# A planner's durations set anew, and five key chunks moved from VectorE to ScalarE, in a 32-head attention kernel

## The chip, the core and the metric

One core of one Trainium2 chip. The metric is the device time of one execution in microseconds; of several executions, the median. The profiled execution is one more, with a time of its own.

## What is computed

Attention over 32 heads with 2048 queries and 2048 keys of 20 numbers each, where queries and keys are brought to unit length first and each head has its own temperature `t`:

```python
qn = q / (jnp.sqrt((q * q).sum(axis=-1, keepdims=True)) + eps)
kn = k / (jnp.sqrt((k * k).sum(axis=-1, keepdims=True)) + eps)
logits = jnp.einsum('bhqd,bhkd->bhqk', qn, kn) * t[None, :, None, None]
attn = _softmax(logits, axis=-1)
return jnp.einsum('bhqk,bhkd->bhqd', attn, v)      # q, k, v: (1, 32, 2048, 20) bf16
```

Logits are bounded by `t`, about 1, so the exponential needs no maximum taken off first. A column of ones beside V gives the softmax's sum.

## The kernel before

**Tiles.** The 2048 keys of a head are 16 chunks of 128 keys; the 2048 queries are 4 groups of 512. A unit is one chunk by one query group: a logit tile of 128 x 512 in one PSUM bank. The exponential of a unit is made in one of two ways, and `DVE_TILES` says for how many of a head's 16 chunks each is used (3 and 4 by turns, so 3.5 on average go to VectorE).

**ScalarE's way** (`add_wave`, L406 on). Three units make a wave: TensorE computes its three logit tiles into one half of `psA` (task `qkA`), and one ACTIVATE of 128 x 1536 (L429, task `exp`) writes the exponentials to the ring `p_ring`, which holds 36 units. `psA` has two halves, so the logits of a wave may be computed once the ACTIVATE two waves back has ended. Of a wave's three matmuls the first two use 64 rows of the array each and run side by side; the third uses 128 rows.

**VectorE's way** (`add_dtile`, L444 on). One chunk, four query groups. Four times, TensorE computes one logit tile into `psD`, a single bank (task `qkD`), and VectorE turns it into 16-bit integers (task `t1`, L457, tile `xt`); `psD` is free for the next only then. After that VectorE makes from the whole `xt` (128 x 2048) the three parts of an approximate exponential: `ee` (L462), `ss` (L465), and `mm` then `tt` (L467, L470). TensorE multiplies all three by V.

**Output.** For four units (one chunk) TensorE adds V times the exponentials into `psO`: four matmuls of 32 columns side by side (L378; tasks `pvA` from the ring, `pvE`, `pvS`, `pvT` from VectorE's tiles). `psO` is one bank for all heads: when a head's products are all in, VectorE transposes it (`tr`, L387), and only then may the next head's first product be issued. VectorE divides by the sum (L391, L392), SyncE stores.

**Preparation.** For each head VectorE squares, sums, takes a reciprocal root and scales (L286 to L308), SyncE transposes and copies with DMAs.

**What sets the order.** All work is a list of tasks, each with an engine, a duration in us, its predecessors and a priority (lower is sooner). `Program.schedule` plays the list in time: an engine that is free takes the ready task of the lowest priority number, and holds it for its duration; a successor on another engine becomes ready after `SEM_LAT` of the engine it waits for. The order found is then fixed: each engine issues its tasks in it, and waits on semaphores where a task needs another engine. So a duration in that list does no work on the chip; it only decides what stands ahead of what. Waves have the priority `due - 100`, `qkD` `due - 50`, `t1` `due - 5`, V products and the rest about `due`, where due is counted in heads.

Durations before, for the tasks that the change touches: a wave's logits `0.22 * max(1, len(us) - 1)` = 0.44, a `psD` tile 0.22, a V product `PE_GROUP` = 0.27, an ACTIVATE `0.093 + n / 1200` = 1.373, the three large preparation steps 0.75 each.

Of the kernel before, what the change touches and what calls it, by code (L numbers as in the profile page):

```python
# [14 lines left out]
ACT = mybir.ActivationFunctionType  # L15
# [24 lines left out]
class Program:  # L40

    SEM_LAT = {"PE": 0.20, "ACT": 0.15, "DVE": 0.10, "POOL": 0.15, "SP": 0.0}

    def __init__(self):
        self.tasks = []
# [5 lines left out]

    def schedule(self):
        for t in self.tasks:
            t.n, t.users = 0, []
        for i, t in enumerate(self.tasks):
            t.seq = i
            t.deps = list(dict.fromkeys(t.deps))
            t.n = len(t.deps)  # L60
            for d in t.deps:
                d.users.append(t)
        free = {}
        ready = {}
        events = []
        rt = {}

        def arrive(t, when):
            heapq.heappush(events, (when, 0, t.seq, t))

        for t in self.tasks:
            free.setdefault(t.eng, 0.0)
            ready.setdefault(t.eng, [])
            rt[t.seq] = 0.0
            if t.n == 0:
                arrive(t, 0.0)
        order = {e: [] for e in free}
        done = 0
        while events:
            now = events[0][0]  # L80
            touched = set()
            while events and events[0][0] <= now:
                _, kind, _, t = heapq.heappop(events)
                touched.add(t.eng)
                if kind == 0:
                    heapq.heappush(ready[t.eng], (t.pri, t.seq, t))
            for e in touched:
                if free[e] > now + 1e-9 or not ready[e]:
                    continue
                _, _, t = heapq.heappop(ready[e])  # L90
                t.start = now
                t.end = now + t.dur
                free[e] = t.end
                order[e].append(t)
                done += 1
                heapq.heappush(events, (t.end, 1, t.seq, t))
                for u in t.users:
                    lat = t.lat if t.dma else (0.0 if u.eng == e and e != "DVE" else self.SEM_LAT[e])
                    rt[u.seq] = max(rt[u.seq], t.end + lat)
                    u.n -= 1  # L100
                    if u.n == 0:
                        arrive(u, rt[u.seq])
        assert done == len(self.tasks), "dependence cycle"
        self.order = order
        return order
# [57 lines left out]
def bass_standalone__qk_norm__prompt_kernel(  # L163
# [7 lines left out]
    B, H, S, D = q.shape  # L171
    assert B == 1 and D == 20 and S == 2048, (B, H, S, D)
    R = S // 128
# [3 lines left out]
    NB = 4  # L177
    NT = 3
    NX = 3
    DVE_TILES = [4 if h % 2 else 3 for h in range(H)]  # L180
    WPLAIN = 5
    PE_GROUP = 0.27
    SH_ENG, SH_DUR = "DVE", 0.60

    with ExitStack() as es:
# [78 lines left out]
        def add_prep(h):  # L264
            b, b2, bt = h % NB, h % 2, h % NT
            due = h - 2.2
            war = ([norm[h - NB]] if h >= NB else []) + ([trn[h - 2]] if h >= 2 else [])
            lds = []
            for nh in range(4):
                src = bass.AP(q.tensor, q[0, h].offset + nh * D,  # L270
                              [[16 * D, 32], [4 * D, 4], [512 * D, 4], [1, D]])
                dst = qk_sb[b][32 * nh:32 * nh + 32, 0:R, :].rearrange("p (c g) d -> p c g d", g=4)
                lds.append(add("ACT" if h == 0 and nh >= 2 else "SP", f"ldq{h}", lambda eng, tk, dst=dst, src=src: eng.dma_start(dst, src),
                               0.6, war, due - 0.5 + 0.01 * (nh >= 2), lat=2.5, dma=f"q{b}a" if h == 0 and nh >= 2 else f"q{b}"))
            src_k = k[0, h].rearrange("(p r) d -> p r d", p=128)
            lds.append(add("SP", f"ldk{h}", lambda eng, tk: eng.dma_start(qk_sb[b][:, R:2 * R, :], src_k),
                           0.6, war, due - 0.51, lat=2.5, dma=f"k{b}"))
            src_v = v[0, h].rearrange("(p r) d -> p r d", p=128)
            warv = pv_users[h - NB] if h >= NB else z_v[b]
            ld_v[h] = add("SP", f"ldv{h}", lambda eng, tk: eng.dma_start(vaug[b][:, :, 0:D], src_v),  # L280
                          0.6, warv, due - 0.4, lat=3.0, dma=f"v{b}")

            def dv(name, fn, dur, deps):
                return add("DVE", name + str(h), fn, dur, deps, due)
            x = qk_sb[b]
            c = [dv("sq", lambda eng, tk: eng.tensor_tensor(sq[:, :, :], x[:, :, :], x[:, :, :], ALU.mult),  # L286
                    0.75, lds + prep_deps)]
            c.append(dv("sum", lambda eng, tk: eng.tensor_reduce(rs["sum"][:, :], sq[:, :, :], AXIS_X, ALU.add),  # L288
                        0.75, [c[-1]]))
            c.append(dv("rs", lambda eng, tk: eng.tensor_scalar(  # L290
                rs["u"][:, :].bitcast(I32), rs["sum"][:, :].bitcast(I32), -0.5, 1597463007.0, ALU.mult, ALU.add),
                0.12, [c[-1]]))
            cur = rs["u"]
            for tgt in (rs["y"], rs["r"]):
                c.append(dv("rs", lambda eng, tk, cur=cur: eng.tensor_tensor(  # L295
                    rs["a"][:, :], cur[:, :], cur[:, :], ALU.mult), 0.12, [c[-1]]))
                c.append(dv("rs", lambda eng, tk: eng.scalar_tensor_tensor(  # L297
                    rs["b"][:, :], rs["a"][:, :], -0.5, rs["sum"][:, :], ALU.mult, ALU.mult), 0.12, [c[-1]]))
                c.append(dv("rs", lambda eng, tk, cur=cur, tgt=tgt: eng.scalar_tensor_tensor(
                    tgt[:, :], rs["b"][:, :], 1.5, cur[:, :], ALU.add, ALU.mult), 0.12, [c[-1]]))  # L300
                cur = tgt
            c.append(dv("rs", lambda eng, tk: eng.tensor_scalar(
                rs["r"][:, 0:R], rs["r"][:, 0:R], t_f32[:, h:h + 1], None, ALU.mult), 0.12, [c[-1], tcp]))
            if h == 0:
                first_head(x, c[-1])
                return
            war = [trn[h - 2]] if h >= 2 else [z_qkn[b2]]
            norm[h] = dv("norm", lambda eng, tk: eng.tensor_tensor(  # L308
                qkn[b2][:, :, 0:D], x[:, :, :], bc(rs["r"][:, :], 2 * R), ALU.mult), 0.75, [c[-1]] + war)
            prep_deps[:] = [norm[h]]  # L310

            war = (qk_users[h - NT] + [*rot[h - NT]] + (qz0 if h == NT else [])) if h >= NT else []
            trn[h] = add("SP", f"trn{h}", lambda eng, tk: eng.dma_start_transpose(
                qkT[bt][:, :].rearrange("p (c n) -> p c n", n=128),
                qkn[b2][:, :, :].rearrange("p r d -> p (r d)")), 0.1, [norm[h]] + war, due + 0.1,
                lat=3.0, dma=f"T{bt}")
            rot[h] = []
            for g in range(NG):
                rot[h].append(add("SP", f"qz{h}", lambda eng, tk, g=g: eng.dma_start(
                    qz[bt][32 * g:32 * g + 32, g, :], qkT[bt][32 * g:32 * g + 32, 0:512]), 0.6,  # L320
                    [trn[h], z_qz[bt]], due + 0.15, lat=2.0, dma=f"Z{bt}"))
            for dl in range(1, 4):
                n = 128 - 32 * dl
                for (d0, s0, m) in ((0, 32 * dl, n), (n, 0, 32 * dl)):
                    rot[h].append(add("SP", f"rot{h}", lambda eng, tk, d0=d0, s0=s0, m=m, dl=dl: eng.dma_start(
                        kR[bt][d0:d0 + m, dl - 1, :], qkT[bt][s0:s0 + m, 512:1024]), 0.6, [trn[h]], due + 0.2,
                        lat=2.0, dma=f"R{bt}"))
# [78 lines left out]
        def add_wave(w):  # L406
# [13 lines left out]
            deps = [act.get(w - 2)]  # L420
            for h in hs:
                deps += [trn[h]] + (rot[h] if w else rot[h][:1]) + (qz0 if w >= WPLAIN and h == 0 else [])
            qk = add("PE", f"qkA{w}", f_qk, 0.22 * max(1, len(us) - 1), deps, due_a(us[0]) - 100)
            for h in hs:
                qk_users[h].append(qk)
            p0 = us[0] % NP
# [1 line left out]
            war = [pv_of_group[(u - NP) // 4] for u in us if u >= NP]  # L428
            act[w] = add("ACT", f"exp{w}", lambda eng, tk: eng.activation(  # L429
                p_ring[:, p0 * 512:p0 * 512 + n], psA[:, slot * WAVE * 512:slot * WAVE * 512 + n], ACT.Exp),  # L430
                0.093 + n / 1200.0, [qk] + war, 0)

        def add_group(i):
            us = list(range(4 * i, 4 * i + 4))
# [9 lines left out]
        def add_dtile(j):  # L444
# [7 lines left out]
            for ii in range(NG):  # L452
                g = NG - 1 - ii
                dep = [trn[h]] + rot[h] + [t1_prev[0]] + (qz0 if h == 0 and j > 0 else [])
                qk = add("PE", f"qkD{j}.{g}", lambda eng, tk, g=g: qk_mm(eng, h, r, g, psD[:, :], 32 if j == 0 else 128), 0.22, dep, due - 50)
                qk_users[h].append(qk)
                t1 = add("DVE", f"t1.{j}.{g}", lambda eng, tk, g=g: eng.tensor_scalar(  # L457
                    xt[s][:, 512 * g:512 * g + 512], psD[:, :], X_MUL, X_ADD, ALU.mult, ALU.add), 0.60,
# [103 lines left out]
```

## Time and profile before

| | |
|---|---|
| median of 2 runs | 788.19 us (788.02 to 788.36) |
| the profiled execution's own time | 787.52 us |
| its span (first to last instruction) | 785.4 us |
| granted TensorE clock | 0.996 of full |
| PE (TensorE matmul) busy | 718.6 us, 91% |
| DVE (VectorE) busy | 752.7 us, 96% |
| ACT (ScalarE) busy | 736.4 us, 94% |
| DMA engines' mean busy share, 100 to 200 us | 0.30 |

A profile's row names the engine, the line, the operation and the tiles. Two instructions of one engine overlap in it: the next may start before the one before has been acknowledged. So the start-to-start distance of two neighbours (here called the pitch) is shorter than the duration of one, and a busy sum, in which overlaps count once, holds a little waiting that no row calls idle. A matmul's row is its latency; its pitch is less.

### The profile page before, as it was taken

The page shows a single profiled execution, that of the slowest core. Times are in us where ns is not written, and L with a number is a line of the kernel's source. Part 1 is how long each engine was busy: PE and PEld are TensorE (multiplying, and loading weights), DVE is VectorE, ACT ScalarE, POOL GpSimd, SP SyncE. Part 2 cuts the span into 40 slices and gives each one's busy share as a digit, 9 for nine tenths or more (in the row PEclk, how much of TensorE's full clock was granted, in tenths as well). Part 3 has the DMA queues.
Part 4 walks back from the last instruction along what each step waited for, and adds up shares of the span by engine and source line. Part 5 has one row for each costly group of instructions (what it writes and reads, how often), then busy time and mean ns, then how long its engine had stood idle before and what let it go on. Part 6 is the DMA issues. An engine that isn't in the chain of part 4 may idle for free.

```text
span 785.4 us, 12656 instructions
## 1 busy us (share of the span) xinstructions
PE 718.6 (91%) x4992; PEld 201.1 (26%) x4992; DVE 752.7 (96%) x1355; ACT 736.4 (94%) x536; POOL 5.5 (1%) x16
## 2 busy tenths in 40 slices
PE   0999999999999999999999999999999999999996
PEld 0222222222222222222222222222222222222221
DVE  6799999999999999999999999999999999999998
ACT  1899999999999999999999999999999999999994
POOL 2000000000000000000000000000000000000000
PEclk9999999999999999999999999999999999999998
DMA  7324132232323233132332323223232331321100
GB/s 82 50 40 71 42 52 40 46 52 54 55 38 47 43 53 58 40 53 28 57 53 50 54 31 58 41 50 59 30 53 45 54 58 32 46 43 44 42 5 9
DMA packets 199466, 36.49 MB, mean 46 GB/s; under 512 B 175216, under 2 KB 199408, under 8 KB 199408
## 3 DMA queue, kind: packets, MB, share of 16 engines
q1 hardware_dynamic: 198352, 35.66, 28.0%
q8 instruction: 39, 0.64, 0.3%
q10 hardware_dynamic: 1056, 0.04, 0.1%
q14 instruction: 19, 0.16, 0.1%
HBM read 7.87 MB, written 2.62 MB: 13 GB/s over the span
## 4 chain that ended last, share of the span: by engine, by line
DVE 58%; PE 37%; issue 3%; DMA 1%; SPq 0%; DVEq 0%
DVE xt L457 23%; PE psA L369 16%; PE psO L378 14%; DVE tt L470 12%; PE psD L369 8%; DVE mm L467 6%; DVE ss L465 5%; DVE ee L462 4%; DVE sq L286 2%; DVE qkn L308 2%; DVE o_stage L392 1%; DVE oT L387 1%; DVE rs_a L295 1%; DVE rs_sum L288 1%; DVE rs_b L297 1%
## 5 line engine op out<-in xcount | busy, mean ns | idle before, releaser
L429 ACT ACTIVATE p_ring<-psA 128x1536 bf16<-128x1536 f32 x534 | 734.9, 1457 | 37.4 <-PE psA L369 32.5
L457 DVE TENSOR_SCALAR xt<-psD 128x512 int16<-128x512 f32 x448 | 307.7, 687 | 27.3 <-PE psD L369 22.4
L369 PE MATMUL psA<-qz,kR 64*128 64x512 bf16 (+1 forms) x1189 | 314.0, 389 | 1.2 <-ACT p_ring L429 0.2
L378 PE MATMUL psO<-p_ring,vaug 128*32 128x512 bf16 x1600 | 145.4, 387 | 2.5 <-DVE oT L387 2.4
L369 PE MATMUL psD<-qz,kR 128*128 128x512 bf16 x333 | 129.2, 388 | 17.9 <-DVE xt L457 14.1
L470 DVE TENSOR_TENSOR tt<-xt,mm 128x2048 f16<-128x2048 f16 x112 | 136.5, 1219 | 0.1
L369 PEld LDWEIGHTS psA<-qz,kR 64*128 64x128 bf16 (+1 forms) x1189 | 82.1, 94 | 196.3 <-issue 162.1
L369 PE MATMUL psA<-qz,qkT 64*128 64x512 bf16 (+1 forms) x396 | 129.9, 388 | 0.3
L462 DVE TENSOR_SCALAR ee<-xt 128x2048 int16<-128x2048 int16 x112 | 77.0, 687 | 0.2
L465 DVE TENSOR_SCALAR ss<-xt 128x2048 int16<-128x2048 int16 x112 | 77.1, 688 | 0.0
L467 DVE TENSOR_SCALAR mm<-xt 128x2048 int16<-128x2048 int16 x112 | 76.9, 687 | 0.0
L369 PEld LDWEIGHTS psD<-qz,kR 128*128 128x128 bf16 x333 | 32.0, 96 | 98.2 <-DVE xt L457 72.1
L378 PEld LDWEIGHTS psO<-p_ring,vaug 128*32 128x32 bf16 x1600 | 36.6, 94 | 75.3 <-issue 63.2
L378 PE MATMUL psO<-tt,vaug 128*32 128x512 f16 x448 | 44.8, 390 | 8.0 <-DVE tt L470 3.6
L369 PE MATMUL psD<-qz,qkT 128*128 128x512 bf16 x111 | 43.0, 388 | 7.6 <-DVE xt L457 5.2
L378 PE MATMUL psO<-ee,vaug 128*32 128x512 f16 x448 | 44.7, 389 | 3.7 <-DVE ee L462 3.4
L378 PE MATMUL psO<-ss,vaug 128*32 128x512 f16 x448 | 44.8, 390 | 3.4 <-DVE ss L465 2.4
L369 PEld LDWEIGHTS psA<-qz,qkT 64*128 64x128 bf16 (+1 forms) x396 | 31.5, 94 | 63.7 <-issue 52.6
L286 DVE TENSOR_TENSOR sq<-qk_sb 128x640 f32<-128x640 bf16 x32 | 26.0, 813 | 0.1
L288 DVE TENSOR_REDUCE rs_sum<-sq 128x32 f32<-128x640 f32 x32 | 25.7, 804 | 0.1
L308 DVE TENSOR_TENSOR qkn<-qk_sb,rs_r 128x640 bf16<-128x640 bf16 x31 | 25.3, 816 | 0.0
L387 DVE STREAM_TRANSPOSE oT<-psO 128x512 f32<-128x512 f32 x32 | 22.7, 711 | 0.7 <-PE psO L378 0.7
(37 smaller groups left out, 136.6 us busy)
## 6 DMA issues: line engine op xcount, KB each, us to landing
kR<-qkT SPq DMA_DIRECT2D x62, 96.0 KB, 2.1
qz<-qkT SPq DMA_DIRECT2D x128, 32.0 KB, 1.9
kR<-qkT SPq DMA_DIRECT2D x62, 64.0 KB, 2.0
qk_sb<-in_k_dram SPq DMA_DIRECT2D x32, 80.0 KB, 2.1
vaug<-in_v_dram SPq DMA_DIRECT2D x32, 80.0 KB, 3.3
out_dram<-o_stage SPq DMA_DIRECT2D x32, 80.0 KB, 1.6
qk_sb<-in_q_dram SPq DMA_DIRECT2D x126, 20.0 KB, 2.5
kR<-qkT SPq DMA_DIRECT2D x62, 32.0 KB, 1.9
```

The lines of the kernel that those rows point to most:

```text
L286: c = [dv("sq", lambda eng, tk: eng.tensor_tensor(sq[:, :, :], x[:, :, :], x[:, :, :], ALU.mult), 0.75, lds + prep_deps)]
L288: c.append(dv("sum", lambda eng, tk: eng.tensor_reduce(rs["sum"][:, :], sq[:, :, :], AXIS_X, ALU.add), 0.75, [c[-1]]))
L308: norm[h] = dv("norm", lambda eng, tk: eng.tensor_tensor(qkn[b2][:, :, 0:D], x[:, :, :], bc(rs["r"][:, :], 2 * R), ALU.mult), 0.75, [c[-1] ...
L369: return eng.matmul(dst, lhsT, mov, tile_position=(p0, 0))
L378: last = eng.matmul(psO[32 * g:32 * g + 32, :], lhsT(g), rhs_of(g), start=start, stop=False, skip_group_check=True, tile_position=(0, 32 * g))
L387: tr = add("DVE", f"tr{h}", lambda eng, tk: eng.transpose(oT[:, :, :].rearrange("p r d -> p (r d)"), psO[:, :]), 0.62, pv_users[h] + ([fin ...
L429: act[w] = add("ACT", f"exp{w}", lambda eng, tk: eng.activation(p_ring[:, p0 * 512:p0 * 512 + n], psA[:, slot * WAVE * 512:slot * WAVE * 5 ...
L457: t1 = add("DVE", f"t1.{j}.{g}", lambda eng, tk, g=g: eng.tensor_scalar(xt[s][:, 512 * g:512 * g + 512], psD[:, :], X_MUL, X_ADD, ALU.mult ...
L462: te = add("DVE", f"e{j}", lambda eng, tk: eng.tensor_scalar(ee[s][:, :], xt[s][:, :], 0x7C00, KE_BITS, ALU.bitwise_and, ALU.bitwise_or), ...
L465: t5 = add(SH_ENG, f"s{j}", lambda eng, tk: eng.tensor_scalar(ss[s][:, :], xt[s][:, :], float(SHIFT - 4096), None, ALU.add), SH_DUR, t1s + ...
L467: tm = add("DVE", f"m{j}", lambda eng, tk: eng.tensor_scalar(mm[s2][:, :], xt[s][:, :], 0x3FF, 0x3800, ALU.bitwise_and, ALU.bitwise_or), 0.60,
L470: tT = add("DVE", f"T{j}", lambda eng, tk: eng.tensor_tensor(tt[s][:, :], xt[s][:, :].bitcast(FP16), mm[s2][:, :].bitcast(FP16), ALU.mult) ...
```

## The change

Three VectorE chunks in two of three heads and four in the third (heads 1, 4, ... 31) instead of three and four by turns: 107 chunks in place of 112 on VectorE, 405 in place of 400 on ScalarE. All other edits are durations of the planner: a wave's logits 0.55 (0.24 in the first five waves), a `psD` tile 0.24, a V product 0.23, and 0.09 more for a TensorE task that is of another kind than the one before it, where kind is the first two letters of the task's name (`qk` or `pv`); an ACTIVATE `0.065 + n / 1200` = 1.345; the three large preparation steps 0.86; TensorE's latency 0.18. A predecessor may now be a function that gives a list; no task has one.

```diff
-    SEM_LAT = {"PE": 0.20, "ACT": 0.15, "DVE": 0.10, "POOL": 0.15, "SP": 0.0}
+    SEM_LAT = {"PE": 0.18, "ACT": 0.15, "DVE": 0.10, "POOL": 0.15, "SP": 0.0}
...
-            t.deps = list(dict.fromkeys(t.deps))
+            deps = []
+            for d in t.deps:
+                deps += d() if callable(d) else [d]
+            t.deps = list(dict.fromkeys(deps))
...
+        last_pe = [""]
...
                 t.end = now + t.dur
+                if e == "PE":
+                    kind = t.name[:2]
+                    if kind != last_pe[0]:
+                        t.end += 0.09
+                    last_pe[0] = kind
                 free[e] = t.end
...
-    DVE_TILES = [4 if h % 2 else 3 for h in range(H)]
+    DVE_TILES = [4 if h % 3 == 1 else 3 for h in range(H)]
     WPLAIN = 5
-    PE_GROUP = 0.27
+    PE_GROUP = 0.23
...
             c = [dv("sq", lambda eng, tk: eng.tensor_tensor(sq[:, :, :], x[:, :, :], x[:, :, :], ALU.mult),
-                    0.75, lds + prep_deps)]
+                    0.86, lds + prep_deps)]
             c.append(dv("sum", lambda eng, tk: eng.tensor_reduce(rs["sum"][:, :], sq[:, :, :], AXIS_X, ALU.add),
-                        0.75, [c[-1]]))
+                        0.86, [c[-1]]))
...
-                qkn[b2][:, :, 0:D], x[:, :, :], bc(rs["r"][:, :], 2 * R), ALU.mult), 0.75, [c[-1]] + war)
+                qkn[b2][:, :, 0:D], x[:, :, :], bc(rs["r"][:, :], 2 * R), ALU.mult), 0.86, [c[-1]] + war)
...
-            qk = add("PE", f"qkA{w}", f_qk, 0.22 * max(1, len(us) - 1), deps, due_a(us[0]) - 100)
+            qk = add("PE", f"qkA{w}", f_qk, 0.24 if w < WPLAIN else 0.55 if len(us) > 1 else 0.24, deps, due_a(us[0]) - 100)
...
-                0.093 + n / 1200.0, [qk] + war, 0)
+                0.065 + n / 1200.0, [qk] + war, 0)
...
-                qk = add("PE", f"qkD{j}.{g}", lambda eng, tk, g=g: qk_mm(eng, h, r, g, psD[:, :], 32 if j == 0 else 128), 0.22, dep, due - 50)
+                qk = add("PE", f"qkD{j}.{g}", lambda eng, tk, g=g: qk_mm(eng, h, r, g, psD[:, :], 32 if j == 0 else 128), 0.24, dep, due - 50)
```

What it does to the order is shown at two places on TensorE. The first is where `psO` passes from head 10 to head 11. A row `psA` belongs to a wave (three matmuls in all), `psD` is one tile for VectorE, `psO` is a V product; `vaug3` is V of head 11, `vaug2` of head 10, and a number behind a name is a buffer's. Before:

```order
L378 MATMUL psO<-tt1,vaug2 32x512 x4
L369 MATMUL psD<-qz2,kR2 128x512
L369 MATMUL psA<-qz2,kR2 128x512 x3
L378 MATMUL psO<-p_ring,vaug3 32x512 x12
L369 MATMUL psD<-qz2,qkT2 128x512
L369 MATMUL psA<-qz2,qkT2 128x512
L369 MATMUL psA<-qz2,kR2 128x512 x2
L378 MATMUL psO<-p_ring,vaug3 32x512 x4
L378 MATMUL psO<-ee2,vaug3 32x512 x4
```

And with the change (lines of the changed kernel are 9 higher here):

```order
L387 MATMUL psO<-tt0,vaug2 32x512 x4
L378 MATMUL psA<-qz2,qkT2 128x512
L378 MATMUL psA<-qz2,kR2 128x512 x2
L378 MATMUL psD<-qz2,kR2 128x512
L387 MATMUL psO<-p_ring,vaug3 32x512 x4
L378 MATMUL psA<-qz2,kR2 128x512 x3
L387 MATMUL psO<-ee1,vaug3 32x512 x4
L387 MATMUL psO<-p_ring,vaug3 32x512 x4
L378 MATMUL psD<-qz2,qkT2 128x512
L378 MATMUL psA<-qz2,kR2 128x512 x2
```

Before, three V products of the new head and a `psD` tile stand between one wave and the next; with the change, one V product and one `psD` tile, and the products that were held back follow after later waves, three passes at a time.

The second place is TensorE's end. Before:

```order
L369 MATMUL psD<-qz1,kR1 128x512
L369 MATMUL psA<-qz1,qkT1 128x512
L378 MATMUL psO<-p_ring,vaug3 32x512 x4
L378 MATMUL psO<-ss2,vaug3 32x512 x4
L369 MATMUL psD<-qz1,kR1 128x512
L378 MATMUL psO<-p_ring,vaug3 32x512 x4
L369 MATMUL psD<-qz1,kR1 128x512
L378 MATMUL psO<-tt2,vaug3 32x512 x4
L378 MATMUL psO<-ee0,vaug3 32x512 x4
L378 MATMUL psO<-ss0,vaug3 32x512 x4
L378 MATMUL psO<-tt0,vaug3 32x512 x4
```

With the change:

```order
L378 MATMUL psD<-qz1,kR1 128x512
L378 MATMUL psA<-qz1,kR1 128x512 x2
L378 MATMUL psA<-qz1,qkT1 128x512
L378 MATMUL psA<-qz1,kR1 128x512 x2
L378 MATMUL psA<-qz1,qkT1 128x512
L387 MATMUL psO<-p_ring,vaug3 32x512 x4
L387 MATMUL psO<-ee1,vaug3 32x512 x4
L387 MATMUL psO<-ss1,vaug3 32x512 x4
L387 MATMUL psO<-p_ring,vaug3 32x512 x8
L387 MATMUL psO<-tt1,vaug3 32x512 x4
```

Before, two `psD` tiles and then all of the last chunk's VectorE work follow the last wave; with the change the last `psD` tile stands ahead of the last two waves.

More of the change, by code (lines that the diff above doesn't have):

```diff
@@ L55, in schedule @@
         for t in self.tasks:
-            t.n, t.users = 0, []
+            t.users = []
         for i, t in enumerate(self.tasks):
             t.seq = i
-            t.deps = list(dict.fromkeys(t.deps))
+            deps = []
+            for d in t.deps:
+                deps += d() if callable(d) else [d]
+            t.deps = list(dict.fromkeys(deps))
             t.n = len(t.deps)
```

## The prediction

> **What bounds the kernel now.** I read the page first: span, busy times, the chain that ended last, the costliest groups.
>
> ```profile
> span 785.4 us, 12656 instructions
> PE 718.6 (91%) x4992; PEld 201.1 (26%) x4992; DVE 752.7 (96%) x1355; ACT 736.4 (94%) x536; POOL 5.5 (1%) x16
> DVE 58%; PE 37%; issue 3%; DMA 1%; SPq 0%; DVEq 0%
> L429 ACT ACTIVATE p_ring<-psA 128x1536 bf16<-128x1536 f32 x534 | 734.9, 1457 | 37.4 <-PE psA L369 32.5
> L457 DVE TENSOR_SCALAR xt<-psD 128x512 int16<-128x512 f32 x448 | 307.7, 687 | 27.3 <-PE psD L369 22.4
> ```
>
> Three engines stand above 90%, and the chain goes to and fro between VectorE and TensorE. ScalarE does not appear in it, yet is 94% busy. So no busy sum alone gives the end; each engine's own work has to be set beside the span.
>
> ScalarE first. The timeline of its first microseconds, and a dense stretch:
>
> ```profile
> 16.41 1.45 ACT L429 ACTIVATE p_ring<-psA 128x1536 bf16<-128x1536 f32 x1 [13.37 <-PE psA L369]
> 19.15 5.62 ACT L429 ACTIVATE p_ring<-psA 128x1536 bf16<-128x1536 f32 x4 [1.29 <-PE psA L369]
> 25.47 1.45 ACT L429 ACTIVATE p_ring<-psA 128x1536 bf16<-128x1536 f32 x1 [0.70 <-PE psA L369]
> 28.19 4.13 ACT L429 ACTIVATE p_ring<-psA 128x1536 bf16<-128x1536 f32 x3 [1.26 <-PE psA L369]
> ```
>
> Three neighbours take 4.13 and one alone 1.45, so the pitch of a fed ScalarE is (4.13 - 1.45) / 2 = 1.34 us; neighbours overlap by 0.11. The first wave starts at 16.41, and the seventh at 28.19: 11.78 us for six pitches (8.04), so the start loses 3.7 us. The end:
>
> ```profile
> 772.07 3.28 ACT L429 ACTIVATE p_ring<-psA 128x1536 bf16<-128x1536 f32 x3
> 775.41 0.40 PE L378 MATMUL psO<-p_ring,vaug 128*32 128x512 bf16 x4
> 777.90 0.69 DVE L462 TENSOR_SCALAR ee<-xt 128x2048 int16<-128x2048 int16 x1
> 778.51 0.69 DVE L465 TENSOR_SCALAR ss<-xt 128x2048 int16<-128x2048 int16 x1
> 779.11 0.69 DVE L467 TENSOR_SCALAR mm<-xt 128x2048 int16<-128x2048 int16 x1
> 779.83 1.22 DVE L470 TENSOR_TENSOR tt<-xt,mm 128x2048 f16<-128x2048 f16 x1
> 781.78 0.72 DVE L387 STREAM_TRANSPOSE oT<-psO 128x512 f32<-128x512 f32 x1 [0.72 <-PE psO L378]
> 783.34 0.33 SPq L395 DMA_DIRECT2D out_dram<-o_stage  x1
> ```
>
> The last ACTIVATE ends at 775.35 and the span at 785.4: a tail of 10.0 us in which VectorE finishes its last chunk alone. Between 16.41 and 775.35 lie 758.9 us; 533 waves at 1.34 and a last short one of 0.6 need 714.8. So ScalarE is late by 44 us in all, 3.7 at the start and about **40 later**. The short wave's row in the groups, and two rows of the view of waits, which show only half of this:
>
> ```profile
> L429 ACT ACTIVATE p_ring<-psA 128x512 bf16<-128x512 f32 x1 | 0.6, 606 | 0.0
> ...
> ACT p_ring L429 <- PE psA L369: 32.5, 65, 13.4
> PEld psD L369 <- DVE xt L457: 100.0, 246, 1.7
> ```
>
> 32.5 less the 13.4 before the first wave is 19; the rest are waves late by less than the overlap of 0.11 and that overlap lost.
>
> Why the waves are late, at the place that the order's first piece shows:
>
> ```profile
> 283.32 4.27 ACT L429 ACTIVATE p_ring<-psA 128x1536 bf16<-128x1536 f32 x3
> 285.40 0.71 PE L369 MATMUL psA<-qz,kR 64*128 64x512 bf16 x3
> 286.04 0.83 PE L378 MATMUL psO<-p_ring,vaug 128*32 128x512 bf16 x12
> 286.80 0.39 PE L369 MATMUL psD<-qz,qkT 128*128 128x512 bf16 x1
> 287.13 0.71 PE L369 MATMUL psA<-qz,kR 64*128 64x512 bf16 x2
> 287.77 0.40 PE L378 MATMUL psO<-p_ring,vaug 128*32 128x512 bf16 x4
> 287.88 5.48 ACT L429 ACTIVATE p_ring<-psA 128x1536 bf16<-128x1536 f32 x4 [0.28 <-PE psA L369]
> 288.00 0.39 PE L378 MATMUL psO<-ee,vaug 128*32 128x512 f16 x4
> 288.32 0.39 PE L369 MATMUL psA<-qz,qkT 64*128 64x512 bf16 x1
> 288.64 0.39 PE L369 MATMUL psA<-qz,kR 128*128 128x512 bf16 x1
> 288.87 0.38 PE L369 MATMUL psD<-qz,kR 128*128 128x512 bf16 x1
> ```
>
> Pitches of TensorE's passes: 0.23 between two V products (287.77 to 288.00) and from a wave's third matmul to a `psD` tile (288.64 to 288.87), both of one array shape; 0.32 wherever the shape changes (288.00 to 288.32; 288.32 to 288.64; 286.80 to 287.13). A wave costs 0.64. From its first matmul to its ACTIVATE go 0.75 (287.13 to 287.88). Its half of `psA` came free when the ACTIVATE two back ended, 0.11 after the last one's start; so of 1.34 about **0.43 us** are to spare before ScalarE waits. Here the ring's ACTIVATE began at 286.14 (287.59 less 1.45), the wave could have gone at about 286.3, but three V products and a `psD` tile stood ahead: it went at 287.13, and ScalarE lost 0.4. The old plan had priced a wave at 0.44 and no change of shape, so it saw time there for four passes. The second kind of lateness is a wait for VectorE in front of the wave:
>
> ```profile
> 402.30 0.10 PEld L378 LDWEIGHTS psO<-ss,vaug 128*32 128x32 bf16 x4 [0.41 <-DVE ss L465]
> 402.63 0.39 PE L369 MATMUL psA<-qz,kR 64*128 64x512 bf16 x2
> 403.38 6.84 ACT L429 ACTIVATE p_ring<-psA 128x1536 bf16<-128x1536 f32 x5 [0.24 <-PE psA L369]
> ```
>
> TensorE issues in order, so a V product that waits 0.41 for `ss` holds the wave behind it.
>
> **The change part by part.** *Five chunks to ScalarE.* VectorE's pitches:
>
> ```profile
> 403.43 0.82 DVE L286 TENSOR_TENSOR sq<-qk_sb 128x640 f32<-128x640 bf16 x1
> 404.16 0.69 DVE L457 TENSOR_SCALAR xt<-psD 128x512 int16<-128x512 f32 x1
> 404.76 1.22 DVE L470 TENSOR_TENSOR tt<-xt,mm 128x2048 f16<-128x2048 f16 x1
> 405.90 0.69 DVE L457 TENSOR_SCALAR xt<-psD 128x512 int16<-128x512 f32 x1
> 406.50 0.71 DVE L387 STREAM_TRANSPOSE oT<-psO 128x512 f32<-128x512 f32 x1
> ```
>
> 0.60 for `xt`, 1.14 for `tt`, and 0.60 for each of `ee`, `ss`, `mm` (777.90 to 778.51 to 779.11). A chunk is 7 x 0.60 + 1.14 = 5.34; VectorE loses 26.7 us of work. ScalarE gets 20 units: 540 full waves at 1.34 are 723.6, 8.8 more than its 714.8. ScalarE thus becomes the engine with the longest own way: 16.41 + 3.7 + 723.6 + 0.1 = 743.8 before tail and lateness.
>
> *TensorE's work.* Counted in the two orders, with a wave as two passes and four V matmuls as one: before 2251 passes with 1852 changes of shape, after 2234 with 1780. At 0.32 and 0.23 that is 684 and 674 us: 10 less, no bound of itself.
>
> *The new order.* By the same prices the stretch from one wave to the next has four passes besides the wave 46 times before, 3 times after. Two waves in a row need more than 2 x 1.34 + 0.4 us of TensorE 45 times before and never after; three in a row 56 times and once. So lateness of the first kind should nearly go: the 0.43 to spare covers what is left. Its bounds: if every wave's own overrun counted, with no slack (40.9 us in the old order, 26.1 in the new), the 40 would fall to 25.7; if both kinds go, since VectorE has 26.7 us less to do and is waited for less, to some 5. Of the late waves that I followed, two in three were of the first kind; I take one third of 40, **14 us**.
>
> *Tail.* The last `psD` tile now stands ahead of the last two waves, so VectorE's last chunk (0.43 for the tile, an `xt`, three times 0.60, 1.22) runs beside two ACTIVATEs instead of behind them. What stays is 0.05 from the ACTIVATE to its product, 0.23 for one behind it, 0.40 for that, 1.56 from transposition to store (781.78 to 783.34) and 2.06 for the store: 4.3. I take **5**, between 4.3 and the old 10.
>
> *At nothing:* ring and loads; SyncE's steps keep their number per head, and no wave after the start waits for a DMA in the view of waits. The preparation's 0.86 is longer than its pitch (`sq` 0.73, 403.43 to 404.16); VectorE will be ahead of the plan by 0.4 us a head, on which nothing hangs.
>
> **Sum.** 743.8 + 14 + 5 = 762.8 us of span. The profiled execution took 2.1 more than its span (787.52 to 785.4), and the median is 0.7 above it: **765.6 us**, 2.9% less. Its own bounds: 743.8 + 5 + 4.3 = 753 to 743.8 + 25.7 + 10 = 779.5 of span.
>
> The Trainium skill's page "ScalarE: Activation LUTs" (section "What ACT_TABLE_LOAD costs") gives 186 ns + 0.833 ns an element, with neighbours overlapping by 93 ns: an estimate from it is a pitch of 1.37, the sum 18 us longer. This case's rows have 1.45 and 1.34 for the same shape, and they decide.
>
> **Rivals.** *VectorE remains last.* It carried 58% of the chain; then the span falls by its work alone, 785.4 - 26.7 = 758.7, **761.5 us**. Against it: ScalarE's 743.8 plus a tail leaves little room below. Chance 0.13.
>
> *TensorE paces.* It waits for both others and both wait for it; if its order and not ScalarE is what the rest follows, the gain is its 10 us: 785.4 - 10 = 775, **778 us**. For it: 246 waits of `psD` for `xt`, which stay, since `psD` is still one bank. Against: no stretch of its own work exceeds ScalarE's pace by the slack. Chance 0.21.
>
> *ScalarE is bound, and as late as before: slower.* The plan charges 0.24 for a `psD` tile ahead of a wave and sees no change of kind, but the rows have 0.33 (286.80 to 287.13): a `psD` tile stands right ahead of a wave 231 times, so TensorE falls behind the plan by 0.09 x 231 = 21 us, which puts waves behind it. With the 40 us of lateness kept and the tail as it was, 743.8 + 40 + 10 = 793.8, **796.6 us**. It decides from a lateness of 36.6 with the short tail on (785.4 - 743.8 - 5). Against: the count above has that 0.32 in it. Chance 0.08. The Trainium skill's "TensorEngine Tiling (Array Packing)", section "Key Properties", says that changing the tiling mode, not only the tile, drains TensorE; the trace's 0.32 against 0.23 agrees, and by that rule the plan's two kinds are too few.
>
> *The change does nothing:* excluded, the orders differ from the first chunk on.
>
> **How the numbers follow.** The forecast's case has the remaining 0.58. Two per cent, about what a measurement of this kernel can tell from no change, is 15.8 us: 772.4 and 804. Faster by more: 0.55 of the forecast's case (all but a lateness above 21) and 0.12 of VectorE's, 0.67. Within: 0.03, 0.01, TensorE's 0.21 and 0.05 of the slow case, 0.30. Slower: 0.03. Range 754 to 781: it holds the forecast's bounds nearly whole and both nearer rivals, and leaves out the slow case.
>
> **What would show it.** Right: ScalarE's waiting for `psA` falls from 32.5 to 25 or less (13.4 of it before the first wave); no tail over 6 us; VectorE's busy sum falls by 5 x 6.0 to about 722; ScalarE's rows in long unbroken runs. TensorE's case: VectorE idle before `xt` grows above 40 us, with ScalarE still waiting about 30. Wrong altogether: ScalarE's waits stay above 32 with the tail short.

## The result, and the profile after

The changed kernel takes **751.53 us** (median of 2 runs, 751.18 to 751.88), 0.9535 of before (95% interval 0.9494 to 0.9576). The forecast was 765.6 in a range of 754 to 781: the direction was right, the gain of 4.65% larger than the range allowed. The profiled execution took 751.88 with a span of 750.1.

The page of the changed kernel, in the rows that answer to those shown of before (lines are 9 higher):

```profile
span 750.1 us, 12494 instructions
PE 697.3 (93%) x4952; PEld 191.7 (26%) x4952; DVE 724.1 (97%) x1315; ACT 727.6 (97%) x542; POOL 5.5 (1%) x16
ACT 95%; PE 2%; DVE 1%; DMA 1%; SPq 0%; ACTq 0%; issue 0%; DVEq 0%
L438 ACT ACTIVATE p_ring<-psA 128x1536 bf16<-128x1536 f32 x540 | 726.1, 1608 | 16.4 <-PE psA L378 16.4
L466 DVE TENSOR_SCALAR xt<-psD 128x512 int16<-128x512 f32 x428 | 292.8, 684 | 19.0 <-PE psD L378 15.4
```

The chain that ended last has changed hands: ScalarE, absent from it before, now holds 95% of it. ScalarE's busy sum is 8.8 us lower than before (736.4 to 727.6) with 6.67 waves more to do: a busy sum counts each lost overlap as work, and before many were lost. VectorE's sum falls by 28.6 (forecast some 30). ScalarE's timeline shows what happened in its last row:

```profile
16.49 1.45 ACT L438 ACTIVATE p_ring<-psA 128x1536 bf16<-128x1536 f32 x1 [13.46 <-PE psA L378]
19.11 5.62 ACT L438 ACTIVATE p_ring<-psA 128x1536 bf16<-128x1536 f32 x4 [1.17 <-PE psA L378]
25.43 1.45 ACT L438 ACTIVATE p_ring<-psA 128x1536 bf16<-128x1536 f32 x1 [0.70 <-PE psA L378]
27.92 717.65 ACT L438 ACTIVATE p_ring<-psA 128x1536 bf16<-128x1536 f32 x534 [1.03 <-PE psA L378]
```

From 27.92 to 745.57 ScalarE never stands: 534 waves without a gap, (717.65 - 1.45) / 533 = 1.344 us each. The start loses 3.4 us (3.7 before); the lateness after it, 40 us before, is zero. Next is the place where `psO` passes from head 10 to head 11, whose rows before showed a wave 0.8 us behind three V products and a `psD` tile (only TensorE's matmuls, with one row of ScalarE):

```profile
275.03 7.04 ACT L438 ACTIVATE p_ring<-psA 128x1536 bf16<-128x1536 f32 x5
276.76 0.71 PE L378 MATMUL psA<-qz,kR 64*128 64x512 bf16 x2
277.31 0.38 PE L378 MATMUL psD<-qz,kR 128*128 128x512 bf16 x1
277.75 0.40 PE L387 MATMUL psO<-p_ring,vaug 128*32 128x512 bf16 x4
278.10 0.71 PE L378 MATMUL psA<-qz,kR 64*128 64x512 bf16 x3
278.75 0.40 PE L387 MATMUL psO<-ee,vaug 128*32 128x512 f16 x4
278.97 0.39 PE L387 MATMUL psO<-p_ring,vaug 128*32 128x512 bf16 x4
279.29 0.39 PE L378 MATMUL psD<-qz,qkT 128*128 128x512 bf16 x1
279.62 0.39 PE L378 MATMUL psA<-qz,kR 64*128 64x512 bf16 x2
```

The waves start at 276.76, 278.10 and 279.62; of the ring's products that were held back, one goes between each two of them. The waits (us in total, times, longest), the first row of the kernel before and the others of the changed one:

```profile
PEld psA L369 <- ACT p_ring L429: 45.3, 156, 0.6
...
PEld psA L378 <- ACT p_ring L438: 167.6, 450, 0.9
PEld psD L378 <- DVE xt L466: 35.5, 100, 1.7
ACT p_ring L438 <- PE psA L378: 16.4, 4, 13.5
```

TensorE now waits for ScalarE (45.3 us in 156 waits before, 167.6 in 450 now), and for VectorE's `xt` a third as long as before (100.0). ScalarE's four waits are those of the start. The end, with the last `psD` tile as its first row:

```profile
741.65 0.39 PE L378 MATMUL psD<-qz,kR 128*128 128x512 bf16 x1
...
744.74 1.23 DVE L479 TENSOR_TENSOR tt<-xt,mm 128x2048 f16<-128x2048 f16 x1
745.62 0.40 PE L387 MATMUL psO<-p_ring,vaug 128*32 128x512 bf16 x4 [0.85 <-ACT p_ring L438]
746.02 0.40 PE L387 MATMUL psO<-tt,vaug 128*32 128x512 f16 x4
746.47 0.72 DVE L396 STREAM_TRANSPOSE oT<-psO 128x512 f32<-128x512 f32 x1 [0.51 <-PE psO L387]
748.03 0.33 SPq L404 DMA_DIRECT2D out_dram<-o_stage  x1
```

The last `tt` ends at 745.97, 0.4 after the last ACTIVATE: the tail is 4.5 us (10.0 before).

### The profile page after: what moved, and what is told of

It reads as the page before. It is cut to its first block, busy times and chain, and to the rows that moved or that the text cites. A ratio compares the mean times of both kernels' runs of the same rounds, so it can differ in the third digit from the quotient of the medians.

```text
span 750.1 us, 12494 instructions
## 1 busy us (share of the span) xinstructions
PE 697.3 (93%) x4952; PEld 191.7 (26%) x4952; DVE 724.1 (97%) x1315; ACT 727.6 (97%) x542; POOL 5.5 (1%) x16
## 4 chain that ended last, share of the span: by engine, by line
ACT 95%; PE 2%; DVE 1%; DMA 1%; SPq 0%; ACTq 0%; issue 0%; DVEq 0%
ACT p_ring L438 95%; PE psA L378 1%; DMA kR<-kx 1%; PE psO L387 1%; PE psD L378 0%; DMA qk_sb<-in_q_dram 0%; DVE rs_sum L297 0%; DVE sq L295 0%; ACTq L194 0%; DVE kx L349 0%; DVE rs_b L306 0%; DVE rs_a L304 0%; SPq L282 0%; DVE oT L396 0%; DVE xt L466 0%
## 5 line engine op out<-in xcount | busy, mean ns | idle before, releaser
L438 ACT ACTIVATE p_ring<-psA 128x1536 bf16<-128x1536 f32 x540 | 726.1, 1608 | 16.4 <-PE psA L378 16.4
L378 PE MATMUL psA<-qz,kR 64*128 64x512 bf16 (+1 forms) x1204 | 318.6, 389 | 18.0 <-ACT p_ring L438 13.3
L466 DVE TENSOR_SCALAR xt<-psD 128x512 int16<-128x512 f32 x428 | 292.8, 684 | 19.0 <-PE psD L378 15.4
L387 PE MATMUL psO<-p_ring,vaug 128*32 128x512 bf16 x1620 | 155.4, 388 | 1.0 <-ACT p_ring L438 0.9
L479 DVE TENSOR_TENSOR tt<-xt,mm 128x2048 f16<-128x2048 f16 x107 | 130.2, 1217 | 0.1
L378 PE MATMUL psD<-qz,kR 128*128 128x512 bf16 x318 | 122.5, 385 | 2.4 <-DVE xt L466 1.1
L471 DVE TENSOR_SCALAR ee<-xt 128x2048 int16<-128x2048 int16 x107 | 73.4, 686 | 0.2
L474 DVE TENSOR_SCALAR ss<-xt 128x2048 int16<-128x2048 int16 x107 | 73.3, 685 | 0.0
L476 DVE TENSOR_SCALAR mm<-xt 128x2048 int16<-128x2048 int16 x107 | 73.3, 685 | 0.0
L387 PEld LDWEIGHTS psO<-p_ring,vaug 128*32 128x32 bf16 x1620 | 39.3, 94 | 85.7 <-issue 73.7
```

Source lines behind the costliest of these rows:

```text
L378: return eng.matmul(dst, lhsT, mov, tile_position=(p0, 0))
L387: last = eng.matmul(psO[32 * g:32 * g + 32, :], lhsT(g), rhs_of(g), start=start, stop=False, skip_group_check=True, tile_position=(0, 32 * g))
L471: te = add("DVE", f"e{j}", lambda eng, tk: eng.tensor_scalar(ee[s][:, :], xt[s][:, :], 0x7C00, KE_BITS, ALU.bitwise_and, ALU.bitwise_or), ...
L474: t5 = add(SH_ENG, f"s{j}", lambda eng, tk: eng.tensor_scalar(ss[s][:, :], xt[s][:, :], float(SHIFT - 4096), None, ALU.add), SH_DUR, t1s + ...
L476: tm = add("DVE", f"m{j}", lambda eng, tk: eng.tensor_scalar(mm[s2][:, :], xt[s][:, :], 0x3FF, 0x3800, ALU.bitwise_and, ALU.bitwise_or), 0.60,
L479: tT = add("DVE", f"T{j}", lambda eng, tk: eng.tensor_tensor(tt[s][:, :], xt[s][:, :].bitcast(FP16), mm[s2][:, :].bitcast(FP16), ALU.mult) ...
```

## The experiments

Twelve kernels test two readings of the gain: theory O, that the new order stopped making waves late, and theory V, that the lighter load on VectorE did. Each ratio is to runs of the kernel before on the same chip. For each, "lateness" is the last ACTIVATE's end less the first one's start, less 1.344 for each full wave and its own time for a last short one, with the start's 3 to 4 us in it; "tail" is from the last ACTIVATE's end to the span's end; the last column is the view's wait of `psD`'s weight loads for `xt`. "Pairs over" counts in the order, priced at 0.32 and 0.23 as in the prediction, how often two waves in a row need over 0.4 us more of TensorE than ScalarE takes for them; for e2 to e6, e8 and e10 the expectations have this count, for the others it was not on record ahead of the run.

| kernel | chunks | median us | ratio (95%) | pairs over | lateness | tail | `psD` for `xt` |
|---|---|---|---|---|---|---|---|
| before | 112 | 788.19 | | 45 | 41.9 | 10.0 | 100.0 |
| the change | 107 | 751.53 | 0.9535 (0.9494 to 0.9576) | 0 | 3.2 | 4.5 | 35.5 |
| e1 new durations alone | 112 | 796.31 | 1.0097 (1.0080 to 1.0114) | 22 | 43.8 | 18.8 | 66.2 |
| e2 fewer chunks alone | 107 | 783.76 | 0.9939 (0.9924 to 0.9954) | 39 | 34.3 | 4.1 | 99.4 |
| e3 TensorE's durations old | 107 | 762.51 | 0.9670 (0.9656 to 0.9685) | 6 | 13.2 | 4.4 | 71.4 |
| e4 no charge for kind | 107 | 759.16 | 0.9629 (0.9614 to 0.9643) | 8 | 10.4 | 4.1 | 62.1 |
| e5 ACTIVATE's duration old | 107 | 756.29 | 0.9598 (0.9584 to 0.9612) | 5 | 7.0 | 4.1 | 69.8 |
| e6 e2 with ACTIVATE's new | 107 | 766.83 | 0.9730 (0.9716 to 0.9745) | 16 | 18.6 | 4.3 | 88.3 |
| e7 | 109 | 764.84 | 0.9706 (0.9692 to 0.9720) | 6 | 9.5 | 14.6 | 46.3 |
| e8 all old | 96 | 824.78 | 1.0451 (1.0407 to 1.0495) | 22 | 61.9 | 4.1 | 101.3 |
| e9 all new | 96 | 785.51 | 0.9975 (0.9954 to 0.9997) | 0 | 21.5 | 4.1 | 69.8 |
| e10 charge by shape | 107 | 755.39 | 0.9586 (0.9573 to 0.9599) | 0 | 2.5 | 8.0 | 33.0 |
| e11 e1, `psD` first | 112 | 790.61 | 1.0027 (1.0017 to 1.0038) | 31 | 35.3 | 18.6 | 57.5 |
| e12 | 108 | 766.73 | 0.9728 (0.9714 to 0.9741) | 5 | 9.1 | 15.3 | 48.8 |

**e1, the new durations alone.** From the changed kernel:

```diff
-    DVE_TILES = [4 if h % 3 == 1 else 3 for h in range(H)]
+    DVE_TILES = [4 if h % 2 else 3 for h in range(H)]
```

> The new durations, but 112 chunks on VectorE as before. Theory O (the order made the waves late): most of the gain is here already. VectorE has 26.7 us more work than in the changed kernel, so it may pace: 751.5 + 26.7 = 778 if VectorE had no room there, down to 742 (ScalarE's 533 waves at 1.344, start 20, tail 4.5) if it had; I expect 755 to 765. Theory V (VectorE's relief did it): most of the gain is missing, 775 to 788, and ScalarE waits for its logits about 30 us or more in the view of waits.

796.31: both theories missed, the new durations alone lose 1%. Its waits and, below them, pieces of ScalarE's timeline and of the tail:

```profile
PEld psD L378 <- DVE xt L466: 66.2, 156, 1.8
ACT p_ring L438 <- PE psO L387: 35.8, 13, 6.9
ACT p_ring L438 <- PE psA L378: 18.2, 7, 13.7
...
654.95 44.44 ACT L438 ACTIVATE p_ring<-psA 128x1536 bf16<-128x1536 f32 x33 [2.84 <-PE psO L387]
702.23 45.87 ACT L438 ACTIVATE p_ring<-psA 128x1536 bf16<-128x1536 f32 x34 [2.84 <-PE psO L387]
...
782.50 0.69 DVE L471 TENSOR_SCALAR ee<-xt 128x2048 int16<-128x2048 int16 x1
788.83 0.69 DVE L471 TENSOR_SCALAR ee<-xt 128x2048 int16<-128x2048 int16 x1
```

The waves are no longer late for their logits (18.2 us, 13.7 of it before the first). ScalarE runs 33 waves without a gap, and then stands for V products that free its ring (35.8 us in 13 waits; with 112 chunks in the old order it was 0.5 us, by the view of waits of before). VectorE with 112 chunks is behind, `psO` cannot pass to the next head before its parts are in, the ring fills; and at the end VectorE still makes two chunks alone. In place of late logits, late V products now hold ScalarE up.

**e2, fewer chunks alone.** From the kernel before:

```diff
-    DVE_TILES = [4 if h % 2 else 3 for h in range(H)]
+    DVE_TILES = [4 if h % 3 == 1 else 3 for h in range(H)]
```

> 107 chunks on VectorE, but the old durations. In its order 39 pairs of neighbouring waves need over 0.4 us more TensorE work than ScalarE takes (45 before the change, none after). Theory O: the lateness of about 40 us stays nearly whole, 748 + 30 to 40 = 778 to 788. Theory V: VectorE is waited for less and the lateness goes, 752 to 760.

783.76, as theory O has it and outside theory V's numbers. The waits, the first row of the kernel before and the others of e2:

```profile
PEld psO L378 <- DVE tt L470: 31.7, 83, 1.8
...
PEld psD L369 <- DVE xt L457: 99.4, 256, 1.7
PEld psO L378 <- DVE tt L470: 8.5, 24, 1.0
DVE oT L387 <- PE psO L378: 28.3, 4, 17.2
ACT p_ring L429 <- PE psA L369: 26.8, 41, 14.3
```

VectorE has time: its last transposition waits 17.2 us for V products. Waits of V products for `tt` have shrunk from 31.7 to 8.5, so these went with VectorE's load; but lateness falls by 8 us only, and the waits of `psD` for `xt` are what they were, 99.4 against 100.0, with 26.7 us less of VectorE's work. **Alone, one half of the change is worth 4.4 us, the other costs 8; together they bring 36.7.**

**e3, TensorE's durations old; e4, no charge for a change of kind.** From the changed kernel; e4 is the first line of e3's edit alone:

```diff
-                        t.end += 0.09
+                        t.end += 0.0
...
-    SEM_LAT = {"PE": 0.18, "ACT": 0.15, "DVE": 0.10, "POOL": 0.15, "SP": 0.0}
+    SEM_LAT = {"PE": 0.20, "ACT": 0.15, "DVE": 0.10, "POOL": 0.15, "SP": 0.0}
...
-    PE_GROUP = 0.23
+    PE_GROUP = 0.27
...
-            qk = add("PE", f"qkA{w}", f_qk, 0.24 if w < WPLAIN else 0.55 if len(us) > 1 else 0.24, deps, due_a(us[0]) - 100)
+            qk = add("PE", f"qkA{w}", f_qk, 0.22 * max(1, len(us) - 1), deps, due_a(us[0]) - 100)
```

(and 0.22 for 0.24 in a `psD` tile.)

> The changed kernel with only TensorE's durations as they were (wave 0.44, psD tile 0.22, V product 0.27, no 0.09 for a change of kind, latency 0.20); the ACTIVATE's 1.345 and the preparation's 0.86 stay new. Six pairs of waves need over 0.4 us too much, against 39 with all durations old. Theory O by that count: a lateness of 3 to 8 us, 755 to 760; the name of the change (TensorE's change between QK and PV) would mean the lateness comes back, 775 to 788. Theory V: 752.

> The changed kernel without the 0.09 for a TensorE task of another kind; all else new. Eight pairs of waves over by 0.4 us. Theory O: 752 to 758. If the charge for the change of kind is what made the order right: 770 or more. Theory V: 752.

762.51 and 759.16: taken back alone, TensorE's durations cost 11 us, and the charge for kind 7.6. Theory O had the direction and was 1 to 2.5 us short in both.

**e5, the ACTIVATE's duration old; e6, that duration alone put into e2.** Edit of e5 (e6 is its reverse in e2's kernel):

```diff
-                0.065 + n / 1200.0, [qk] + war, 0)
+                0.093 + n / 1200.0, [qk] + war, 0)
```

> The changed kernel with only the ACTIVATE's duration as it was (1.373 in the plan, where the chip's pitch is 1.344). Theory O (only TensorE's passes ahead of waves count): five pairs of waves over by 0.4 us, 752 to 756. Theory P (the order fixes the pace: it holds as much VectorE work between two waves as fills the planned pitch, so ScalarE is kept near 1.373): up to 540 x 0.029 = 15.7 us more, 762 to 767.

> The old plan with 107 chunks and only the ACTIVATE's duration new (1.345). With all durations old this took 783.8. Sixteen pairs of waves over by 0.4 us, against 39. Theory O: by that count less than half of the lateness of 33 us, 764 to 768. Theory P: 783.8 - 15.7 = 768. If the preparation's 0.86 made the difference between that kernel and the one with TensorE's old durations (762.5): 780 or more.

756.29 and 766.83. In the old plan the ACTIVATE's price is worth 17 us (783.76 to 766.83), in the new one 4.8. Theory P would have the same 15.7 in both, so it falls as it was put; e6 alone could not tell it from O. With e3 (766.83 to 762.51) the preparation's 0.86 comes to 4.3, though with TensorE's old durations only.

**e7 and e12, one or two chunks back to VectorE.** From the changed kernel, e7 and then e12:

```diff
-    DVE_TILES = [4 if h % 3 == 1 else 3 for h in range(H)]
+    DVE_TILES = [4 if h % 5 in (1, 3) else 3 for h in range(H)]
...
-    DVE_TILES = [4 if h % 3 == 1 else 3 for h in range(H)]
+    DVE_TILES = [4 if h % 3 == 1 or h == 15 else 3 for h in range(H)]
```

> The changed kernel with 109 chunks on VectorE (four in two heads of five). If ScalarE alone is the bound, 2.67 waves fewer: 751.5 - 3.6 = 748. If VectorE has no room left (its work 10.7 us more, and the run with 112 took 796), the ring fills and ScalarE waits for V products: 755 to 770.

> The changed kernel with one chunk more on VectorE (head 15 has four; 108). ScalarE loses 1.33 waves: 751.5 - 1.8 = 749.7 if VectorE has room for one chunk more. If 107 is the edge: 753 to 758, with ScalarE waiting for V products.

764.84 and 766.73. Three rows of ScalarE's timeline in e12, then of VectorE's:

```profile
442.10 45.79 ACT L438 ACTIVATE p_ring<-psA 128x1536 bf16<-128x1536 f32 x34 [0.16 <-PE psO L387]
490.93 67.40 ACT L438 ACTIVATE p_ring<-psA 128x1536 bf16<-128x1536 f32 x50 [3.04 <-PE psO L387]
559.83 189.92 ACT L438 ACTIVATE p_ring<-psA 128x1536 bf16<-128x1536 f32 x141 [1.50 <-PE psO L387]
...
751.28 0.69 DVE L471 TENSOR_SCALAR ee<-xt 128x2048 int16<-128x2048 int16 x1
757.54 0.69 DVE L471 TENSOR_SCALAR ee<-xt 128x2048 int16<-128x2048 int16 x1
```

The ring fills from the middle on, and ScalarE is done at 749.75 with two chunks of VectorE unfinished, as in e1. One chunk of 5.3 us costs 15 us, 11 of it in the tail; 758 was the worst that I had expected. Most of the excess stands in the plan itself. Played through with its own durations (`Program.schedule` alone, without the chip), e12's plan ends at 760.2 us and the changed kernel's at 745.2. These are 15.0 more: VectorE has 5.3 us more to do and stands for 9.6 us more. The chip's spans are 765.0 and 750.1. With the new durations the plans of e7, e10, e12 and the changed kernel end 4.8 to 5.8 us ahead of the chip's spans, e11's 6.4, e1's 10 (786.0 for 796.3) and e9's 23, where the chip waits as told under e8 and e9. With TensorE's old durations the plan of e3 also ends at 745.2, and the chip takes 759.9. Why the priorities leave VectorE standing there is open. And e7, with one chunk more than e12, is 1.9 us faster, so it is the place of a chunk as well as the number. Going up, 107 is the edge; nothing between 96 and 107 was run.

**e8 and e9, three chunks in every head**, from the kernel before and from the changed one:

```diff
-    DVE_TILES = [4 if h % 2 else 3 for h in range(H)]
+    DVE_TILES = [3 for h in range(H)]
...
-    DVE_TILES = [4 if h % 3 == 1 else 3 for h in range(H)]
+    DVE_TILES = [3 for h in range(H)]
```

> All durations old, three chunks in every head (96 on VectorE, 58.7 us less of its work than with 107): VectorE is no bound whatever. ScalarE has 554.7 waves: 16.5 + 3.5 + 745.5 + 5 = 770.5 before lateness. Theory O: 22 pairs of waves still over by 0.4, lateness 15 to 25, 788 to 798. Theory V (waits for VectorE make the lateness): it goes, 771 to 776.

> All durations new, three chunks in every head (96 on VectorE). ScalarE has 14.67 waves more than in the changed kernel. If it is the bound and never late: 751.5 + 14.67 x 1.344 = 771.2. With the old durations the same split took 824.8, 34 us of it in waits of psD tiles for the key copies of the next head; if those waits come from the split (VectorE ahead, the copies late), they are here too, 790 to 800; if from the old plan, they are gone.

824.78 is slower than either theory had it; 785.51 lies between e9's two forecasts. Of e8's waits:

```profile
PEld psD L369 <- DVE xt L457: 101.3, 254, 1.7
PEld psD L369 <- DMA kR<-qkT: 33.9, 20, 3.6
```

and of e9's:

```profile
PEld psD L378 <- DVE xt L466: 69.8, 190, 1.8
PEld psD L378 <- DMA kR<-qkT: 18.0, 17, 2.1
```

Theory V fails again: with 16 chunks less on VectorE, some 85 us of its work, TensorE waits for `xt` as long as before (101.3, 100.0). But these two runs have a wait that no other has. VectorE, with less to do, runs further ahead in the order (in e8 the first `psD` tile of head 12 stands between waves of head 10), and such a tile stands ahead of waves and waits for its own head's rotated keys. Taking the waits off as if all had made ScalarE late, e8's lateness is 61.9 - 33.9 = 28 with the start's 3.4 in it, about what O said, and e9's 21.5 - 18.0 = 3.5, the start's alone.

That subtraction is too simple, for the granted TensorE clock falls beside these waits. Three stretches of e8 about such a wait, one of 2.8 us that ended at 276.17 (the view's columns are the stretch, its length, busy times, then PEclk, the DMA share and GB/s):

```profile
262.00:273.00 11.00, 10.35 (x90) 3.12 (x89) 10.15 (x17) 10.92 (x9) 0.00 (x0) 1.00 0.40 67
276.00:282.60 6.60, 6.43 (x23) 1.31 (x23) 2.08 (x3) 3.93 (x3) 0.00 (x0) 0.50 0.26 25
283.00:300.00 17.00, 16.21 (x121) 4.78 (x120) 16.04 (x32) 16.40 (x13) 0.00 (x0) 1.00 0.23 37
```

Ahead of its tail e8 has ten such stretches at half clock, of 3.4 or 6.8 us, and e9 has four, three of them beside such a wait; the change has none. Going wave by wave, e8 loses 57 us after the first 40: 23 in waves that start within 2 us of the end of a wait for keys, 9 more in or just behind the half-clock stretches, and 25 elsewhere, still the upper end of what O said. For e9 it is 6.6, 6.4 and 4.6 us. How much of the first share is the wait's and how much the clock's is open, and so is why the copies come late. The new durations are worth 39 us at this split, too.

**e10, the charge by the array's shape.** A wave is its own kind on arrival, and counts as `qk` after:

```diff
-                    kind = t.name[:2]
+                    kind = "pv" if t.name[:2] == "pv" else "qk" if t.name[:3] == "qkD" else "w"
...
-                    last_pe[0] = kind
+                    last_pe[0] = "qk" if kind == "w" else kind
```

> The changed kernel with the 0.09 charged for every change of the array's shape, so also for a psD tile ahead of a wave, which the new plan prices too low by 0.09 in 231 places. In its order no stretch of one to six waves is over ScalarE's pace by more than 0.3 us. ScalarE has no lateness left to lose after the start: 751.5 within 1. If the unpriced change still cost something through VectorE's waits: 745 to 749.

755.39, a miss by 3.9. ScalarE is as unbroken as in the changed kernel, and its end comes at the same time:

```profile
398.41 346.96 ACT L438 ACTIVATE p_ring<-psA 128x1536 bf16<-128x1536 f32 x258
...
744.72 0.39 PE L378 MATMUL psD<-qz,kR 128*128 128x512 bf16 x1
747.81 1.22 DVE L479 TENSOR_TENSOR tt<-xt,mm 128x2048 f16<-128x2048 f16 x1
```

The last `psD` tile stands behind the last wave, 3.1 us later than in the changed kernel (744.72, 741.65), and the tail is 8.0 instead of 4.5. The better price bought nothing in the middle and lost at the end.

**e11, `psD` tiles ahead of waves**, in e1's kernel:

```diff
-                qk = add("PE", f"qkD{j}.{g}", lambda eng, tk, g=g: qk_mm(eng, h, r, g, psD[:, :], 32 if j == 0 else 128), 0.24, dep, due - 50)
+                qk = add("PE", f"qkD{j}.{g}", lambda eng, tk, g=g: qk_mm(eng, h, r, g, psD[:, :], 32 if j == 0 else 128), 0.24, dep, due - 150)
```

> The run with the new durations and 112 chunks (796.3) with one edit: psD tiles have the priority due - 150, ahead of waves (due - 100). If that run was slow because TensorE served ScalarE's waves first while VectorE was the bound, VectorE's waits for psD go and the time falls to 765 to 780. If VectorE's work alone set it, it stays, 790 to 800.

790.61. The waits for the ring (28.1 us) and the tail (18.6) stay, so TensorE's preference for waves is not what makes 112 chunks slow; 5.7 of the 8 us that e1 lost to the kernel before come back.

None of the twelve beats the changed kernel.

## Why the prediction was wrong

**What held.** The first wave at 16.49 (forecast 16.41), the loss at the start (3.4; 3.7), the pitch (1.344; 1.34), so "16.41 + 3.7 + 723.6 + 0.1 = 743.8" met a last ACTIVATE that ended at 745.57. The tail: 4.5, forecast 5. ScalarE became the engine that sets the end. The first kind of lateness went, as the counts in the order said. The Trainium skill's page "ScalarE: Activation LUTs", section "What ACT_TABLE_LOAD costs", leads to a pitch of 1.37 by an estimate; 534 waves without a gap at 1.344 differ from it.

**The step that failed** is the sentence "I take one third of 40, **14 us**", with its lower bound of 5. It was zero. The span was missed by 12.7 (762.8 against 750.1): these 14 and 0.5 of the tail too much, 1.8 too little up to the last ACTIVATE. The third was the waves that I had found behind a wait for VectorE, and I took these waits for something that VectorE's speed sets and the order leaves alone. e2 and e8 show that they are not: VectorE's work fell by 26.7 and 85 us, and TensorE's waits of `psD` for `xt` stayed at 99.4 and 101.3. The new durations with VectorE's work untouched (e1) took them to 66.2, the change to 35.5. And the share itself came from too few waves: in the whole trace of before, from 30 us on, 115 of the 180 waves that are over 0.05 us late have TensorE waiting for VectorE for 0.2 us or more ahead of them while their half of `psA` is free, and they hold 24.8 of the 39.4 us, nearer two thirds than one. My reading, which no run tests alone: a plan that believes TensorE free too early puts a `psD` tile ahead of a wave at a moment when `xt` isn't done, so the wait is the wrong place in the order once more. The count of pairs, which I used for the first kind alone, in fact goes with the lateness of all the kernels of 107 chunks: 0 pairs 3 us, 5 pairs 7, 6 and 8 pairs 13 and 10, 16 pairs 19, 39 pairs 34.

**The rivals.** *VectorE remains last*, 761.5: no at 107 chunks, yes one chunk above (e12), where ScalarE stands for V products. I had set the two engines' limits side by side and had not asked what VectorE does when it falls behind: the ring of 36 units stops ScalarE, and the tail grows. *TensorE paces*, 778: no; it waits 167.6 us for ScalarE. *As late as before*: the price of a `psD` tile ahead of a wave that the plan lacks is real, and put into the plan (e10) it leaves ScalarE's pace where it was: the slack of 0.43 covers it.

**What was not seen at all** is that the parts need each other. I had credited the order with the lateness and the chunks with ScalarE's place, as two terms of a sum. Apart they give +8 and -4.4 us, together -36.7: with 112 chunks a good order only lets ScalarE run into a full ring, and with 107 the old order keeps ScalarE late while VectorE has time. Why e1 is even slower than before is shown in part: ScalarE's waits for the ring, the tail, and a plan that itself ends at 786.0. That e11 returns 5.7 us says that some of it is VectorE waiting for its tiles; the rest is open.

## To carry to other kernels

Where engines issue in a fixed order, a wait for another engine ahead of critical work may be a fault of the order as much as a slow engine: see whether the wait shrinks when that engine is relieved before taking it for its load. Price each stretch between two instructions of the engine that should be bound, from pitches and not from durations, and count the stretches over its pace plus the buffer's slack; among the kernels of 107 chunks that count went with the lateness. Where the order comes from a plan with true durations, read the plan's own end first: 745.2 for 750.1 here, 760.2 for 765.0 one chunk on. Moving work and mending the order are not two gains to be added: test each alone, and test one step beyond the split, since here one chunk more on VectorE cost 15 us.

## What the runs showed that was not expected

Three chunks on VectorE in every head bring a wait that no other kernel here has, of a `psD` tile for the rotated keys of a later head (33.9 us in 20 waits in e8, 18.0 in 17 in e9), though a copy of them takes the same 1.9 to 2.1 us from issue to landing on the pages of before and after. Beside the ten longest of the 20 waits in e8, those of 1.9 to 3.6 us, the granted TensorE clock falls to 0.50 for 3.4 or 6.8 us, beginning 1.5 to 3.9 us after the wait began; beside the other ten, of 1.6 us at most, it doesn't.
